# Fused linear attention and feed-forward layer on one core: w_in loaded in whole rows, batch loads issued by SyncE, the first batch spread over four engines

## The chip, the core and the metric

The kernel runs on one core of a Trainium2 chip. The metric is the device time of one execution in microseconds (us); the kernel before takes 349.92 us in the median of three runs (343.51 to 350.42). The engines are PE (TensorE, matmuls), DVE (VectorE), ACT (ScalarE), POOL (GpSimd) and SP (SyncE, which only issues transfers); PEld is PE's weight load.

## The reference

Eight batches with eight heads, 576 positions and 64 features per head go through a linear attention, and its 4608 rows of 512 features through a feed-forward layer with 2048 inner features:

```
theta = pi/2 * pos / 576
phi(x) = concat(relu(x) * cos(theta), relu(x) * sin(theta))        # 128 features
kv  = einsum('bhsf,bhsd->bhfd', phi(k), v);   z = sum_s phi(k)
x   = einsum('bhsf,bhfd->bhsd', phi(q), kv) / (phi(q) . z + 1e-6)
h   = x.transpose(0, 2, 1, 3).reshape(4608, 512) @ w_in             # 512 x 2048
out = (h * sigmoid(beta * h)) @ w_out                               # 2048 x 512
```

All inputs and the output are float32; the kernel multiplies in bf16.

## The kernel before, in words

The feed-forward layer runs over nine chunks of 512 rows (`c`), the attention over eight batches (`b`). The work is written out by hand in the order in which each engine shall take it; every engine executes its own instructions in that order and waits on semaphores. One chunk has 32 slots. Slots 0 to 15 are `h_group`: four matmuls into one of two PSUM banks, then one silu on ACT that writes `g_t`. Slots 16 to 31 are `o_part`: four matmuls each with `wout`, four parts to a 128-row output tile, which ACT copies out. Between the slots of chunk `c` the attention of batch `c + 1` is interleaved (`att_units`): relu of q, the turn of q by a transposing transfer (`q_turn_dma`, SP), relu of k, scaling of v by cosine and sine (`v_scale`), the tangent product of the turned q on POOL (`q_tan`), kv products (`kv_mm`) at slot 12, their copies out of PSUM (`kv_take`), num products (`num_mm`) and divisions (`x_div`) at slots 16, 18 and 20, and the turn of x into `xt` by transposing transfers on SP (`x_turn_dma`) one slot later each. DVE is not bound to the slots and runs ahead of PE. Chunk 0 carries batch 1 in the same way, with its turns on PE (the table `early`), and is a different order of the same steps: there the output parts go through all four row tiles before the next quarter of `wout`.

Batch 0 comes ahead of chunk 0; this stretch is called the head. The weights are loaded in it as well: four tiles of w_in and four of w_out, each 1.05 MB in float32, through four staging buffers (`w_stage`), so that a w_out load waits until a cast has emptied a buffer. The tile `win` wants its 512 input features in an order in which partitions 0 to 63 and 64 to 127 hold features of different heads. Before, `load_w` (lines 95 to 99) makes that order in the transfer: four transfers per tile, each of them into 64 partitions; `cast_w` then casts 128 partitions at once. A batch's q, k and v are 1.18 MB each, and two batches' tiles are held at a time (`raw_pool`).

Who issues: SP the first two batches and the weights, ACT the batches from 2 on. In lines 470 to 475 these issues stand on ACT at the start of a chunk; for batch 3 and on:

```
for c in range(1, NTC):
    if c + 2 < B:
        for name in "qvk":
            load_raw(c + 2, name, eng=nc.scalar)
```

A transfer that is issued takes one of eight semaphores in turn, and waits until the transfer that had that semaphore eight issues before has landed.

Of the kernel before, what the change touches and what calls it, by code (L numbers as in the profile page):

```python
# [10 lines left out]
FP32 = mybir.dt.float32  # L11
# [5 lines left out]
P = 128  # L17
# [5 lines left out]
def kernel(  # L23
# [60 lines left out]
    w_in_v = moe_w_in.rearrange("(jp jj g d) f -> jj d jp g f", jp=2, jj=2, g=2)  # L84
# [3 lines left out]
    def load_w(kind, i, f0=0, f1=512):  # L88
# [78 lines left out]
    xs = one.tile([P, 2, NQ, 2 * D], BF16, name="xs")  # L167
# [21 lines left out]
    def sel(jp):  # L189
        return slice(0, 4) if jp is None else slice(2 * jp, 2 * jp + 2)  # L190
# [31 lines left out]
    def q_turn_pe(b, jp, bank):  # L222
# [9 lines left out]
        for step in range(2):  # L232
            for e in range(2):
                i, n0, n1 = parts[e ^ step]
                if e == 0:
                    nc.scalar.copy(qt[:, jp, n0:n1], v2[i])  # L236
                else:
                    tan_mul(nc.vector, qs[:, jp, n0:n1], v2[i], n0, n1)
# [22 lines left out]
    def kv_take(b, jp, bank, both=False):  # L261
        t = kv_out(jp, bank)
        for g in range(2):
            for jj in range(2):
                rows = slice(jj * HP, (jj + 1) * HP)
                o = kv[rows, g, jp, :, jj * E : (jj + 1) * E]
                a = t[rows, g].rearrange("q (s e) -> q s e", s=2)
                if both and g == 1:
                    nc.scalar.copy(o, a)
                else:  # L270
                    nc.vector.tensor_copy(o, a)  # L271
# [242 lines left out]
```

## Time and profile before

| | before |
|---|---|
| median of 3 runs | 349.92 us (343.51 to 350.42) |
| profiled execution | 348.06 us, span 346.3 us |
| mean granted TensorE clock | 0.962 |
| PE busy | 306.4 us (88% of the span) |
| ACT, DVE, POOL busy | 136.2, 125.9, 73.5 us |
| moved by DMA | 53.60 MB |

The span is the time between the first and the last instruction of the profiled execution. "L339" is line 339 of the kernel before. In the chain and in timelines "ACTq" and "SPq" are the instruction queues of an engine while it issues transfers. A note such as [6.88 <-ACT g_t L343] says that the engine had been idle for 6.88 us just before, and that what it waited for was ACT's writing of g_t in line 343.

### The profile page before, as it was taken

Reading aid. Unit: us, or ns where it says so; the run is one execution under the profiler, and the core shown is the slowest. Engines: PE = TensorE matmul, PEld = TensorE weight load, DVE = VectorE, ACT = ScalarE, POOL = GpSimd, SP = SyncE. Lnnn points to the kernel's source line nnn. Section 1 sums busy time; section 2 is a strip of 40 time slices with the busy share of each in tenths; the row PEclk is TensorE's granted clock in tenths of the full one; section 3 lists DMA queues with packets and bytes.
Section 4 is the critical chain, followed back from the end, with each engine's and each line's share of the span. In section 5 each row is a group of like instructions: output and inputs, shape, how many; then the busy total and the mean of one; then the engine's idle time right before and its main releaser. Section 6 shows DMA issues by size and latency. Waiting matters only on the chain.

```text
span 346.3 us, 5863 instructions
## 1 busy us (share of the span) xinstructions
PE 306.4 (88%) x2363; PEld 146.2 (42%) x2390; DVE 125.9 (36%) x332; ACT 136.2 (39%) x209; POOL 73.5 (21%) x83
## 2 busy tenths in 40 slices
PE   5469958828999899979996999899999999999994
PEld 2354434413444345434542444345444544444441
DVE  3871479517239024802480058114902400000000
ACT  6437501505611661256113721463166127516711
POOL 2520000310233601342131503800370120000000
PEclk9789989976999999999998999999999999999998
DMA  7999990389618942595149706960640251032022
GB/s 276 266 217 256 389 377 12 88 306 389 228 37 154 316 163 50 112 305 204 39 105 253 276 18 129 273 251 17 133 112 3 49 113 30 0 70 53 0 60 61
DMA packets 50986, 53.60 MB, mean 155 GB/s; under 512 B 31232, under 2 KB 32272, under 8 KB 50960
## 3 DMA queue, kind: packets, MB, share of 16 engines
q1 hardware_dynamic: 38736, 24.65, 28.4%
q10 hardware_dynamic: 9536, 21.24, 16.7%
q0 software_dynamic: 2688, 7.34, 9.1%
q8 instruction: 18, 0.29, 0.4%
q14 instruction: 8, 0.07, 0.1%
HBM read 36.71 MB, written 9.44 MB: 133 GB/s over the span
## 4 chain that ended last, share of the span: by engine, by line
PE 68%; DMA 17%; ACTq 5%; DVE 3%; issue 2%; SPq 2%; ACT 1%; POOL 1%; POOLq 0%; DVEq 0%
PE ps L352 32%; PE ps L339 28%; DMA w_stage<-in_moe_w_out_dram 8%; PE ps L279 5%; ACTq L78 5%; DMA qt<-qb 4%; DMA raw_k<-in_k_dram 3%; DMA w_stage<-in_moe_w_in_dram 2%; PE ps L256 2%; SPq L97 1%; DVE wout L114 1%; DVE qs L218 1%; ACT g_t L343 1%; SPq L78 1%; POOL qs L218 1%
## 5 line engine op out<-in xcount | busy, mean ns | idle before, releaser
L339 PE MATMUL ps<-xt,win 128*128 128x512 bf16 x576 | 138.4, 387 | 15.4 <-ACT g_t L343 14.3
L352 PE MATMUL ps<-wout,g_t 128*128 128x512 bf16 x550 | 126.4, 380 | 2.5 <-issue 1.6
L343 ACT ACTIVATE g_t<-ps,beta 128x512 bf16<-128x512 f32 x144 | 98.4, 687 | 61.2 <-PE ps L339 47.7
L339 PEld LDWEIGHTS <-win 128*128 128x128 bf16 x576 | 56.3, 99 | 93.4 <-issue 35.9
L352 PEld LDWEIGHTS <-g_t 128*128 128x128 bf16 x576 | 54.6, 98 | 64.8 <-issue 1.2
L366 POOL DMA_DIRECT2D out_dram<-o_sb x56 | 36.2, 650 | 167.2 <-ACT o_sb L362 167.1
L362 ACT COPY o_sb<-ps 128x512 f32<-128x512 f32 x35 | 20.5, 586 | 108.8 <-PE ps L352 108.8
L271 DVE CAST kv<-ps 64x130 bf16<-64x130 f32 x60 | 17.5, 292 | 87.8 <-PE ps L256 86.8
L218 POOL TENSOR_TENSOR qs<-qt,tanr 128x1152 bf16<-128x1152 bf16 x12 | 28.3, 2378 | 35.7 <-DMA qt<-qb 26.9
L360 DVE COPY o_sb<-ps 128x256 f32<-128x256 f32 x1 | 0.4, 425 | 65.5 <-ACT o_sb L359 65.5
L295 DVE TENSOR_TENSOR xs<-ps,rden 128x768 bf16<-128x768 f32 (+1 forms) x27 | 23.4, 868 | 0.9
L279 PE MATMUL ps<-kv,qt 128*64 128x130 bf16 x288 | 21.2, 229 | 1.3 <-DVE kv L271 1.3
L279 PE MATMUL ps<-kv,qs 128*64 128x130 bf16 x288 | 20.6, 228 | 1.1 <-DVE qs L218 0.6
L279 PEld LDWEIGHTS <-qt 128*64 128x64 bf16 x288 | 16.4, 114 | 11.3 <-issue 10.5
L256 PE MATMUL ps<-vb,rk 64*64 64x130 bf16 x576 | 12.7, 235 | 7.6 <-ACT rk L194 4.0
L214 DVE TENSOR_SCALAR vb<-raw_v,cos 128x256 bf16<-128x256 f32 x63 | 17.1, 348 | 3.4 <-DMA raw_v<-in_v_dram 3.4
L279 PEld LDWEIGHTS <-qs 128*64 128x64 bf16 x288 | 16.7, 113 | 1.4 <-DVE qs L218 0.7
L214 DVE TENSOR_SCALAR vb<-raw_v,sin 128x256 bf16<-128x256 f32 x63 | 17.1, 349 | 0.0
L290 DVE TENSOR_TENSOR den<-ps,eps 128x12 f32<-128x12 f32 (+1 forms) x27 | 4.5, 168 | 32.1 <-PE ps L279 32.1
L256 PEld LDWEIGHTS <-rk 64*64 64x64 bf16 x576 | 10.1, 116 | 12.3 <-issue 6.4
L196 DVE TENSOR_SCALAR qb<-raw_q 128x1152 bf16<-128x1152 f32 x15 | 10.7, 753 | 8.1 <-DMA raw_q<-in_q_dram 8.1
L236 ACT COPY qt<-ps 128x640 bf16<-128x640 bf16 (+1 forms) x8 | 4.9, 640 | 22.1 <-PE ps L230 17.8
(51 smaller groups left out, 79.5 us busy)
## 6 DMA issues: line engine op xcount, KB each, us to landing
out_dram<-o_sb POOLq DMA_DIRECT2D x56, 128.0 KB, 2.9
raw_q<-in_q_dram ACTq DMA_DIRECT2D x6, 1152.0 KB, 7.7
raw_v<-in_v_dram ACTq DMA_DIRECT2D x6, 1152.0 KB, 10.5
raw_k<-in_k_dram ACTq DMA_DIRECT2D x6, 1152.0 KB, 12.3
w_stage<-in_moe_w_out_dram SPq DMA_DIRECT2D x4, 1024.0 KB, 14.1
w_stage<-in_moe_w_in_dram SPq DMA_DIRECT2D x12, 256.0 KB, 9.0
out_dram<-o_sb SPq DMA_DIRECT2D x16, 128.0 KB, 2.4
raw_q<-in_q_dram SPq DMA_DIRECT2D x2, 576.0 KB, 4.5
```

Of the source, the lines that this page charges most:

```text
L78: (eng or nc.sync).dma_start(out=raw_tile(b, name)[:, js].rearrange("q j n d -> q j (n d)"), in_=src.rearrange("(j g) (p n) d -> (g p) j ( ...
L214: nc.vector.tensor_scalar(vb[:, n, :, cs, 0:D], rv[:, :, n, :], scalar1=t[:, n : n + 1], scalar2=None, op0=ALU.mult)
L218: eng.tensor_tensor(dst.rearrange("q n (g p) -> q n g p", g=2), src.rearrange("q n (g p) -> q n g p", g=2), tanr[:, n0:n1].unsqueeze(2).to ...
L256: nc.tensor.matmul(t[jj * HP : (jj + 1) * HP, g], lhsT=rk[hs, n, 2 * jp + jj, :], rhs=vb[hs, n, 2 * jp + jj].rearrange("q s e -> q (s e)") ...
L271: nc.vector.tensor_copy(o, a)
L279: nc.tensor.matmul(ps[gs_, bank, i * 2 * E : (i + 1) * 2 * E], lhsT=(qt, qs)[cs][:, jp, n, gs_], rhs=kv[:, g, jp, cs, :], start=(cs == 0), ...
L295: nc.vector.tensor_tensor(xs[:, jps[0] : jps[-1] + 1, 3 * t : 3 * t + 3].rearrange("q s n (j d) -> q s (n j) d", j=2), nv[:, :, :, :, 0:D] ...
L339: nc.tensor.matmul(h_ps, lhsT=win[jt // 4][:, mi, (jt % 4) * P : (jt % 4 + 1) * P], rhs=xt[:, jp, :, g * HP : (g + 1) * HP], start=(mi == ...
L343: nc.scalar.activation(g_t, h_ps, AF.Silu, scale=beta[:, jt : jt + 1])
L352: nc.tensor.matmul(o_ps, lhsT=gs[c, jt][:, tt * P : (tt + 1) * P], rhs=wout[jt // 4][:, jt % 4, :], start=(jt == 0), stop=(jt == JT - 1))
L362: nc.scalar.copy(o_sb, o_ps)
L366: eng.dma_start(out=out_v[bb, n], in_=o_sb[hf * HP : (hf + 1) * HP, :])
```

## The change

- w_in: one transfer per tile, 128 rows at a time as they lie in memory, into 128 partitions. The order that `win` wants is made by the casts: four casts per tile, each of them from 64 partitions of the staging tile to 64 partitions of `win`, two of the four into the other half. Tile 0 is cast by POOL in eight pieces, tiles 1 and 2 by DVE in four, tile 3 by POOL in four (DVE before).
- Batch loads: all on SP. Batch 2 is issued in chunk 0, the others by `load_next` behind the q turn of the batch before.
- The last two w_out tiles are cast by ACT (six of eight pieces) and DVE (two), after the q turns of batch 1.
- `xs` and `xt` have the two column halves (jp) side by side in each block of 64 rows, so that one transfer turns both; the moving operand of the h products changes with it (`xt[:, :, jp, ...]`).
- `kv_take`: two copies for all four parts, in place of eight.
- The head: 29 warm-up matmuls in place of nine; k's relu on ACT ahead of a qt copy, k's second half loaded and cut in two pieces; the first copies of kv on ACT; division of nine blocks at once, its last third on ACT; xt copies on DVE and ACT.

```diff
-    w_in_v = moe_w_in.rearrange("(jp jj g d) f -> jj d jp g f", jp=2, jj=2, g=2)
+    w_in_v = moe_w_in.rearrange("(j p) f -> p j f", p=P)
...
-        for jj in range(2):
-            for jp in range(2):
-                nc.sync.dma_start(
-                    out=st[jj * HP : (jj + 1) * HP, 2 * jp : 2 * jp + 2, f0:f1],
-                    in_=w_in_v[jj, :, jp, :, i * 512 + f0 : i * 512 + f1])
...
+        nc.sync.dma_start(out=st, in_=w_in_v[:, :, i * 512 : (i + 1) * 512])
+
+    def cast_win(i, gj, eng="dve", f0=0, f1=512):
+
+        g, jj = gj
+        o = win[i].rearrange("q (jp g) f -> q jp g f", g=2)[jj * HP : (jj + 1) * HP, :, g, f0:f1]
+        a = stages["in", i].rearrange("q (jp jj) f -> q jp jj f", jj=2)[g * HP : (g + 1) * HP, :, jj, f0:f1]
...
-    xs = one.tile([P, 2, NQ, 2 * D], BF16, name="xs")
+    xs = one.tile([P, NQ, 2, 2 * D], BF16, name="xs")
...
-            xts[c] = xt_pool.tile([P, 2, NB, P], BF16, name="xt", tag="xt")
+            xts[c] = xt_pool.tile([P, NB, 2, P], BF16, name="xt", tag="xt")
...
+    def kv_take(jps, bank, jjs=(0, 1), gs_=(0, 1), eng="dve"):
+        a0, a1 = jps[0], jps[-1] + 1
+        for jj in jjs:
+            rows = slice(jj * HP, (jj + 1) * HP)
+            o = kv[rows, gs_[0] : gs_[-1] + 1, a0:a1, :, jj * E : (jj + 1) * E]
+            a = ps[rows, bank + gs_[0] : bank + gs_[-1] + 1, a0 * 2 * E : a1 * 2 * E]
...
     def x_turn_dma(b, t):
         for c, o, n0, n1 in pieces(b, t):
-            for jp in range(2):
-                nc.sync.dma_start(out=xt_tile(c)[:, jp, o : o + n1 - n0], in_=xs[:, jp, n0:n1].rearrange("q n c -> q (n c)"),
-                                  transpose=True)
+            nc.sync.dma_start(out=xt_tile(c)[:, o : o + n1 - n0].rearrange("q n s c -> q (n s) c"),
+                              in_=xs[:, n0:n1].rearrange("q n s c -> q (n s c)"), transpose=True)
...
-                             rhs=xt[:, jp, :, g * HP : (g + 1) * HP],
+                             rhs=xt[:, :, jp, g * HP : (g + 1) * HP],
...
+    warm_pe(13)
+    take("act", 0)
+    v_scale(0, 1, 0, eng="pool")
+    v_scale(0, 0, 0)
+    k_relu(0, 0, 2, "act")
+    take("dve", 1)
+    take("dve", 0)
+    take("act", 1)
+    kv_mm(0, 0, 6)
...
+    x_rden(1, 0)
+    x_mul(1, 0, 0, 1)
+    x_mul(1, 0, 1, 2)
+    for n in range(6, NQ):
+        x_mul_act(1, 0, n)
+    for f in (0, 256):
+        for gj in GJ:
+            cast_win(0, gj, "pool", f, f + 256)
...
-    cast_w("in", 2)
+    for gj in GJ:
+        cast_win(2, gj)
     load_w("out", 2)
-    cast_w("in", 3)
+    for gj in GJ:
+        cast_win(3, gj, "pool")
     load_w("out", 3)
...
+        13: lambda: (v_scale(1, 0), [v_scale(1, 1, jp, eng="pool") for jp in range(2)]),
+        17: lambda: k_relu(1),
+        20: lambda: (kv_mm(1, 0, 6), kv_mm(1, 1, 6), q_relu(1, 0), kv_take((0, 1), 6), q_relu(1, 1)),
+        22: lambda: q_turn_pe(1, 0, 4),
+        23: lambda: (q_turn_pe(1, 1, 6), cast_wout(2, "aaaa"), cast_wout(3, "aadd")),
...
+        def load_next():
+            for name in "qvk":
+                if b + 1 < B:
+                    load_raw(b + 1, name)
+
         u = [
-            (0, lambda: (q_relu(b, 0), q_relu(b, 1))),
+            (0, lambda: (q_relu(b, 0), q_relu(b, 1), q_turn_dma(b), load_next())),
             (1, lambda: v_scale(b, 0)),
-            (1, lambda: q_turn_dma(b)),
...
+        if slot == 24:
+            for name in "qvk":
+                load_raw(2, name)
...
-    for name in "qvk":
-        load_raw(2, name, eng=nc.scalar)
     for c in range(1, NTC):
-        if c + 2 < B:
-            for name in "qvk":
-                load_raw(c + 2, name, eng=nc.scalar)
```

How the rows of two engines move. On ACT, between two chunks (line 343 or 381 is the silu, 362 or 400 the copy of an output tile, 321 or 360 the copy of a turned x). Before:

```order
L343 ACTIVATE g_t<-ps,beta 128x512 x16
L362 COPY o_sb<-ps 128x512 x4
L78 DMA raw_q<-in_q_dram 128x4x576
L78 DMA raw_v<-in_v_dram 128x4x576
L78 DMA raw_k<-in_k_dram 128x4x576
```

Now, from the end of chunk 0 on:

```order
L400 COPY o_sb<-ps 128x512 x2
L360 COPY xt<-ps 128x256
L360 COPY xt<-ps 128x512
L381 ACTIVATE g_t<-ps,beta 128x512 x16
L400 COPY o_sb<-ps 128x512 x4
```

No issue of a transfer stands between a chunk's copies and the next chunk's silu instructions any more.

On SP, from the first loads to the last w_out load (a piece of the difference; 64x2x512 is 64 partitions with two pieces of 512):

```order
 L78 DMA raw_v<-in_v_dram 128x2x576
-L78 DMA raw_k<-in_k_dram 128x2x576
-L97 DMA w_stage<-in_moe_w_in_dram 64x2x256 x8
-L97 DMA w_stage<-in_moe_w_in_dram 64x2x512 x12
+L78 DMA raw_k<-in_k_dram 128x576 x2
+L95 DMA w_stage<-in_moe_w_in_dram 128x4x512 x4
 L93 DMA w_stage<-in_moe_w_out_dram 128x4x512 x2
+L78 DMA raw_v<-in_v_dram 128x4x576
 L78 DMA raw_k<-in_k_dram 128x4x576
-L78 DMA raw_v<-in_v_dram 128x4x576
 L78 DMA raw_q<-in_q_dram 128x4x576
 L93 DMA w_stage<-in_moe_w_out_dram 128x4x512 x2
```

Twenty transfers of w_in have become four, and batch 1's v has gone ahead of its k. The same place of the changed program with the semaphores that each row waits for (DMAHW4 and so on are the eight semaphores of transfers, Pool counts POOL's instructions):

```order
L95 DMA w_stage<-in_moe_w_in_dram 128x4x512 [waits DMAHW3_49]
L93 DMA w_stage<-in_moe_w_out_dram 128x4x512 [waits DMAHW4_49,DMAHW0_49,Pool_49]
L93 DMA w_stage<-in_moe_w_out_dram 128x4x512 [waits DMAHW5_49,DMAHW3_49,Pool_49]
L78 DMA raw_v<-in_v_dram 128x4x576 [waits DMAHW6_49]
L78 DMA raw_k<-in_k_dram 128x4x576 [waits DMAHW7_49]
```

The first of the two w_out loads takes the buffer of w_in tile 0 and waits for POOL's last cast of it. The second takes the buffer of w_in tile 3 (DMAHW3 is that tile's load) and waits for POOL's last cast of tile 3; before, the second one waited for a cast on DVE.

## Rows read from the trace of the kernel before

**Rows 1.** The page, part 1: span, busy time per engine.
```profile
span 346.3 us, 5863 instructions
PE 306.4 (88%) x2363; PEld 146.2 (42%) x2390; DVE 125.9 (36%) x332; ACT 136.2 (39%) x209; POOL 73.5 (21%) x83
```

**Rows 2.** Busy time by stage: length, engines, PE clock, DMA share, GB/s.
```profile
25.67:70.07 44.40, 37.47 (x305) 18.56 (x309) 25.96 (x61) 17.86 (x29) 3.92 (x8) 0.96 0.70 221
70.07:252.06 181.99, 165.91 (x1346) 77.97 (x1361) 76.29 (x211) 66.01 (x100) 50.62 (x49) 0.96 0.63 180
252.06:284.54 32.48, 32.22 (x271) 15.37 (x272) 6.40 (x17) 13.34 (x20) 8.91 (x10) 1.00 0.30 67
```

**Rows 3.** The chain of waits from 250 us on: start, length, what.
```profile
263.97 1.15 PE ps L256 x72
...
274.12 0.82 PE ps L279 x24
...
284.54 14.63 PE ps L339 x64
...
299.22 10.74 PE ps L352 x49
```

**Rows 4.** Timeline, starts of chunks 1, 2 and 4: start, length, instruction.
```profile
75.31 2.74 ACTq L78 DMA_DIRECT2D raw_k<-in_k_dram  x1
...
78.83 12.75 PE L339 MATMUL ps<-xt,win 128*128 128x512 bf16 x44 [6.88 <-ACT g_t L343]
...
115.67 1.67 PE L339 MATMUL ps<-xt,win 128*128 128x512 bf16 x7 [1.12 <-ACT g_t L343]
...
186.04 1.23 PE L339 MATMUL ps<-xt,win 128*128 128x512 bf16 x4 [2.81 <-ACT g_t L343]
```

**Rows 5.** Busy time in stretches of the first 51 us, columns as in rows 2.
```profile
0.00:4.00 4.00, 0.00 (x0) 0.00 (x0) 1.39 (x7) 2.71 (x4) 2.19 (x11) 1.00 0.45 144
4.00:11.00 7.00, 6.15 (x29) 3.50 (x29) 3.51 (x8) 4.28 (x8) 2.12 (x1) 1.00 1.03 394
12.00:16.00 4.00, 1.21 (x37) 1.09 (x39) 3.23 (x5) 1.86 (x3) 1.78 (x1) 0.58 1.07 207
18.00:31.00 13.00, 10.13 (x136) 6.15 (x133) 7.93 (x22) 6.40 (x11) 1.09 (x2) 0.94 1.05 223
34.00:51.00 17.00, 13.38 (x87) 5.93 (x90) 10.75 (x28) 5.43 (x8) 0.00 (x0) 0.98 1.05 389
```

**Rows 6.** Timeline of SP: the first w_out loads.
```profile
25.62 1.63 SPq L93 DMA_DIRECT2D w_stage<-in_moe_w_out_dram  x2
```

**Rows 7.** Timeline of the head and of chunk 0.
```profile
11.40 2.38 POOL L208 TENSOR_TENSOR vb<-raw_v,sin 128x1152 bf16<-128x1152 f32 x1 [0.81 <-DMA raw_v<-in_v_dram]
...
14.46 1.19 PE L256 MATMUL ps<-vb,rk 64*64 64x130 bf16 x36 [4.01 <-ACT rk L194]
...
48.84 1.30 PE L256 MATMUL ps<-vb,rk 64*64 64x130 bf16 x20 [3.51 <-DVE vb L214]
...
51.80 1.68 DVE L114 TENSOR_SCALAR wout<-w_stage,rbeta 128x512 bf16<-128x512 f32 x4 [0.91 <-DMA w_stage<-in_moe_w_out_dram]
...
69.10 0.51 PE L315 MATMUL ps<-ident,xs 128*128 128x128 bf16 x6 [0.56 <-DVE xs L295]
```

**Rows 8.** The tile qt: its transposing transfers from issue to landing.
```profile
DMA to landing us min/median/max: 5.5/7.2/15.4
```

**Rows 9.** Groups of instructions, 0 to 26 us: count, busy us, mean ns, idle before.
```profile
L208 POOL TENSOR_TENSOR vb<-raw_v,sin 128x1152 bf16<-128x1152 f32 x2 | 4.5, 2247 | 6.2 <-DMA raw_v<-in_v_dram 6.2
L295 DVE TENSOR_TENSOR xs<-ps,rden 128x384 bf16<-128x384 f32 x6 | 3.3, 558 | 0.2
...
L108 POOL CAST win<-w_stage 128x1024 bf16<-128x1024 f32 x2 | 2.4, 1184 | 3.0 <-DMA w_stage<-in_moe_w_in_dram 2.9
...
L110 DVE CAST win<-w_stage 128x2048 bf16<-128x2048 f32 x1 | 1.2, 1227 | 0.0
...
L321 ACT COPY xt<-ps 128x512 bf16<-128x512 bf16 x1 | 0.6, 586 | 0.1
```

More of the change, by code (lines that the diff above doesn't have):

```diff
@@ L231, in q_turn_pe, with take @@
                                  is_transpose=True, start=(n == n0), stop=(n == n1 - 1))
[L232 to L238, printed above, removed]
+        def take(e, i):
+            _, n0, n1 = parts[i]
+            if e == "act":
+                nc.scalar.copy(qt[:, jp, n0:n1], v2[i])
+            else:
+                tan_mul(nc.vector, qs[:, jp, n0:n1], v2[i], n0, n1)
+        if hold:
+            return take
+        for e, i in (("act", 0), ("dve", 1), ("act", 1), ("dve", 0)):
+            take(e, i)
     def q_turn_dma(b):
@@ L248, in kv_out, with kv_mm @@
         return ps[:, bank : bank + 2, jp * 2 * E : (jp + 1) * 2 * E]
-    def kv_mm(b, jp, bank):
+    def kv_mm(b, jp, bank, jjs=(0, 1)):
         t = kv_out(jp, bank)
         for n in range(NQ):
-            for jj in range(2):
+            for jj in jjs:
                 for g in range(2):
@@ L259, in kv_mm @@
                         start=(n == 0), stop=(n == NQ - 1))
[L261 to L271, printed above, removed]
+    def kv_take(jps, bank, jjs=(0, 1), gs_=(0, 1), eng="dve"):
+        a0, a1 = jps[0], jps[-1] + 1
+        for jj in jjs:
+            rows = slice(jj * HP, (jj + 1) * HP)
+            o = kv[rows, gs_[0] : gs_[-1] + 1, a0:a1, :, jj * E : (jj + 1) * E]
+            a = ps[rows, bank + gs_[0] : bank + gs_[-1] + 1, a0 * 2 * E : a1 * 2 * E]
+            o = o.rearrange("q g s c e -> q g (s c) e")
+            a = a.rearrange("q g (s e) -> q g s e", e=E)
+            if eng == "act":
+                nc.scalar.copy(o, a)
+            else:
+                nc.vector.tensor_copy(o, a)
     def num_mm(b, t, jp, bank):
@@ L299, in x_div, with x_rden, x_mul @@
             op=ALU.mult)
+    rdens = {}
+    def x_rden(jp, bank):
+        nv = x_sums(bank, 3)
+        den = small.tile([P, 3, 3, 2], FP32, name="den3", tag="den3")
+        nc.vector.tensor_tensor(
+            den, nv[:, :, :, :, D],
+            eps9.rearrange("q (t i) -> q t i", t=3).unsqueeze(3).to_broadcast([P, 3, 3, 2]), op=ALU.add)
+        rdens[jp] = small.tile([P, 3, 3, 2], FP32, name="rden3", tag="rden3")
+        nc.vector.reciprocal(rdens[jp], den)
+    def x_mul(jp, bank, t0, t1):
+        nv = x_sums(bank, 3)
+        nc.vector.tensor_tensor(
+            xs[:, 3 * t0 : 3 * t1, jp].rearrange("q n (j d) -> q n j d", j=2),
+            nv[:, t0:t1, :, :, 0:D].rearrange("q t i j d -> q t (i j) d") if t1 - t0 > 1 else nv[:, t0, :, :, 0:D],
+            rdens[jp][:, t0:t1].rearrange("q t i j -> q (t i) j").unsqueeze(3).to_broadcast([P, 3 * (t1 - t0), 2, D]),
+            op=ALU.mult)
@@ L301, in pieces, with x_mul_act @@
+    def x_mul_act(jp, bank, n):
+        t, i = divmod(n, 3)
+        nv = x_sums(bank, 3)
+        for jj in range(2):
+            nc.scalar.activation(xs[:, n, jp, jj * D : (jj + 1) * D], nv[:, t, i, jj, 0:D], AF.Copy,
+                                 scale=rdens[jp][:, t, i, jj : jj + 1])
     def pieces(b, t):
@@ L400 @@
[L400 to L413 removed]
+    for t in range(3):
+        num_mm(0, t, 0, 3 + t)
@@ new lines @@
+    kv_mm(0, 1, 6, (0,))
+    kv_mm(0, 1, 6, (1,))
+    warm_pe(3, bank=1)
+    x_rden(0, 3)
+    x_mul(0, 3, 0, 3)
+    kv_take((1,), 6, eng="act")
+    for t in range(3):
+        num_mm(0, t, 1, t)
+    warm_pe(3, bank=6)
+    x_rden(1, 0)
[6 more added lines that the diff above has]
+            cast_win(0, gj, "pool", f, f + 256)
+    x_turn_pe(0, 0, 6, ("dve",))
+    x_turn_pe(0, 1, 7, ("act",))
```

185 lines of the change are left out of this document (82 added, 103 removed).

## The prediction

> **What bounds the kernel now.** I read the page first: the span is 346.3 us and PE is busy for 306.4 us of it [rows 1]. The profiled execution took 348.06 us, so 1.76 us lie outside the span; the median of the runs is 349.92 us, 0.5% above it, and I make the sum against 348.06.
>
> Then the span by stages, cut where a chunk's first h product may start [rows 2]. Chunk 6 (252.06 to 284.54) has the attention of a batch beside it and no load of a batch: 32.48 us, PE busy 32.22. That is PE's own work, as the chain shows: 64 h products in 14.63 us, 72 kv products in 1.15, three times 24 num products in 0.82, and the o products at 10.74 us for 49 [rows 3], 14.0 for 64; together 32.3. Chunks 1 to 5 do the same work in 181.99 us, which is 36.4 each. So they lose 181.99 - 5 x 32.48 = 19.6 us. The head (up to 25.67) and chunk 0 (44.40 us, PE busy 37.47) lose the rest.
>
> What chunks 1 to 5 wait for stands in the timeline of their starts [rows 4]. ACT issues the batch loads in front of the chunk's silu instructions. At the start of chunk 1 six loads keep ACT's queue until 75.31 + 2.74 = 78.05, and PE's next h product waited 6.88 us for g_t, since it has only two PSUM banks for h. In chunk 2 the same wait is 1.12 us, in chunk 4 it is 2.81. A stall is followed by a lower clock: the 44 h products from 78.83 take 12.75 us, against 14.63 for 64 in [rows 3].
>
> The head and chunk 0 are set by transfers, seen in four windows [rows 5]. The batch's first tiles arrive at 394 GB/s, w_out and batch 1 at 389, but the w_in pieces between them at 207 to 223, with the DMA engines equally busy (1.03 to 1.07). The w_in pieces are the ones that write 64 partitions each. They hold back what stands behind them on SP: the first w_out load is issued at 25.62 [rows 6]. In chunk 0 PE then waits 3.51 us for batch 1's v, and the cast of the third w_out tile starts only at 51.80, on landing [rows 7].
>
> **The change, part by part.**
> *Batch loads from ACT to SP.* ACT loses 18 issues, SP gains 18, and loses 22 transposes (44 become 22, each for both column halves). Batch 2's loads now stand right behind the last w_out load, those of batch c+2 behind batch c+1's q transpose. Who is behind them on SP: the xt transposes of slots 17, 19 and 21, and through them the next chunk's h products. The q transpose is asked for as soon as DVE is through with the last batch's divisions, near slot 21, and lands in 5.5 to 15.4 us [rows 8]; the loads behind it are 3.54 MB, 9.1 us at 389 GB/s. From slot 21 to the next chunk's slot 17 are 28 slots, some 28 us, so both end 3 to 13 us before the next xt transpose, and the move costs nothing; if that cover went, each chunk would lose what the transpose is late. PE's 32.48 us stay: 5 x 32.48 in place of 181.99, **-19.6 us**. Bounds: 0 (a new wait takes all) and -20.6 (32.3 us a chunk from the chain).
>
> *w_in in whole rows.* 4.19 MB at 223 GB/s are 18.8 us, at 389 they are 10.8: the stream of transfers ends 8 us earlier, if whole rows move like w_out's. Between 223 and 389 I take 389, since w_out tiles have the same 128 partitions and 2 KB pieces; 223 goes to a rival.
>
> *The casts.* A cast now covers 64 partitions and reads one half while it writes the other. No row shows such a cast. Price by elements per partition: POOL 1184 ns for 1024, DVE 1227 ns for 2048 [rows 9]. Below: nothing beyond the four quarter casts at these rates; above: twice that, if 64 lanes or the crossing cost as much again. I take the first, the nearest row. POOL then needs 8 x 0.59 = 4.7 us for tile 0 and 4 x 1.18 = 4.7 us for tile 3; DVE 2.5 us each for tiles 1 and 2.
>
> *A new wait.* The second w_out load waits, by the order, for POOL's last cast of w_in tile 3. Behind it on SP stand batch 1, w_out 2 and 3, and batch 2. Working: 0.58 MB of the batch are in at 4.0 us (144 GB/s [rows 5]), the rest of 3.54 MB at 394 GB/s by 11.5, the four w_in tiles by 22.3, the first w_out tile by 25.0. A tile lands about 1.4 us after its last byte (estimate: v's second half, due at 10.0 us by the same rate, let POOL start at 11.40 [rows 7]). Tile 3 lands at 23.7, POOL is through at 28.4, bytes flow again at about 29.5, so the stream idles 4.5 us. The remaining 6.68 MB end at 46.7 and land by 48.1. Before, the cast of 51.80 still had a tile behind it: some 5 us gained, not 8.
>
> *The head.* Before, the first kv product waited for rk until 14.46, since ACT took k after its qt copies [rows 7]; now k goes ahead of one, and 13 warm products fill the wait. I expect kv at 12.0 and the products after it at full clock (it was granted 0.58 between 12 and 16 [rows 5], near its lower level, 1.2 GHz). The pair of kv copies per bank, the nine-block divisions (558 ns per three blocks before [rows 9]) and the spread over ACT and DVE save and add about the same. First h product at 23.0 in place of 25.67: **-2.7 us**. Bounds: 0 (the added instructions eat it) and -4 (kv's gain and the clock in full). POOL's casts of tile 0 end at 15.6 + 4.7 = 20.3, before it.
>
> *Chunk 0.* With the first h product at 23.0, PE reaches kv of batch 1 (slot 20) at 23.0 + 14.6 + 5 x 0.89 = 42.0. Batch 1's k lands at 39.7 and POOL's two sine products (2247 ns each [rows 9]) are done at 41.1, so the 3.51 us wait goes. Late next is w_out tile 2: it lands at 45.5, but ACT casts it behind the four qt copies, which PE releases at 45.7 and 47.3; with a DVE step between two of them they end at 48.6, and four casts at 0.59 (ACT's 128x512 copy takes 586 ns [rows 9]) end at 51.0. PE stands at slot 24 from 47.3: 3.7 us. From there 8 x 0.89 of o, 2.5 of num, 1.5 of transposes (three times 0.51 [rows 7]) and 0.6 for a last xt copy give 62.7. Chunk 0 becomes 39.7 us: **-4.7 us**. Bounds: 0 (casts doubled, POOL holding SP) and -8 (no stall at slot 24).
>
> Sum: -19.6 - 2.7 - 4.7 = -27.0, a span of 319.3 and, with the 1.76 us outside, **321.1 us**.
>
> **A rule weighed.** POOL's tile 3 (23.7 to 28.4) and DVE's eight casts of tiles 1 and 2 (from about 24) meet here for the first time: in the trace before, the POOL cast of 1184 ns [rows 9] ran beside DVE instructions that read PSUM. The Trainium skill's "SBUF — State Buffer" (section "Who interferes with whom") says that a VectorE cast in its two-port mode and a GpSimd instruction exclude each other, the loser waiting for the whole instruction; no row here shows it. By the rows the sum is 321.1; by that rule it is rival A's figure.
>
> **The rivals.**
> A. POOL is late: its casts wait for DVE's, or crossing halves costs. For: no row shows either. Against: POOL has only those casts to do there. If all 4.9 us of DVE's casts come in between, or tile 3's casts double, the second w_out load and all behind it come 4.8 us later, and chunk 0 with them: 326.
> B. Whole rows change nothing for w_in, since its rows stay 8 KB apart in HBM, and that, not the 64 partitions, made 223 GB/s. For: w_out and the batches are contiguous in HBM. Against: half of 389 is close to the 207 to 223 seen, which fits a half of something. Tile 3 then lands 8 us later, PE waits some 3 us for it at slot 12, chunk 0 ends at about 72: 72 + 6 x 32.48 + 61.8 (346.3 - 284.54) + 1.8 = 331. The skill's page named above (section "Can I just issue two DMAs to hit both halves?") says that one transfer over all 128 partitions is what reaches every port; that speaks against B.
> C. The wait moves from ACT to SP: loads stand ahead of transposes, and a chunk's xt or qt is late. For: a q transpose took 15.4 us once [rows 8]. Against: it has 15.8 us to slot 16 beyond its head start. If it costs 4 us in each of five chunks: 341, no change that can be told.
> D. Slower: xt now has both column halves side by side, so the h products' moving operand steps 512 bytes between its 128-byte runs, not 256. If that slowed PE's reading, 576 products would pay. To pass 357 from 321 they need +62 ns each (now 14.63 / 64 = 229); it decides from there on. Against: o products read one contiguous run and take 219 [rows 3], so runs with gaps already cost nearly nothing. At +70 ns: 361.
> E. Better: chunk 0 and the head at their lower bounds, -8 and -4: 316.5, or 315.5 with the chunks at 32.3.
>
> **The numbers.** Chances: forecast 0.62, A 0.18, B 0.07, C 0.05, D 0.02, E 0.06. The likeliest is 321.1 us. Its own range is 317 to 326 (above, the head's or chunk 0's gain lost, 2.7 or 4.7; below, most of chunk 0's stall gone). A and B reach to 331, E down to 315; with a microsecond or two at either end for what a term is misjudged by, 314 to 333. The cases in it hold 0.93 by their chances, and I count on some 0.85, for what is unnamed. A measurement here tells some 2% apart, 343 to 357. Faster by more: the forecast, A, B, E and a part of C, 0.95. Within: the rest of C and small losses, 0.03. Slower: D, 0.02.
>
> **What would show it.** In the changed profile: chunks 1 to 5 at 32.5 us each, no wait of h products for g_t over 1 us, no batch load on ACT; w_in at 380 GB/s or more; the first h product near 23; a gap of 4 to 5 us in the transfers before the second w_out tile, its length telling the forecast from A; a PE wait of 3 to 4 us near 47 us for w_out tile 2's casts on ACT. Wrong would be: chunks still at 34 or more, w_in near 220 GB/s, or h products over 240 ns.

## The result: 328.5 us in place of 348.4, with 7.4 us left behind the forecast in one stretch

Timed side by side, the changed kernel takes 328.5 us (median; 328.32 to 329.4) and the kernel before 348.38. The ratio is 0.9522 [0.9438, 0.9605]. The forecast was 321.1. The profiled execution took 329.4 us, 1.9 of it outside the span. Spans below are of one profiled execution each; where the median of the times tells another size, it stands beside.

The page of the changed kernel, part 1, against [rows 1]:

```profile
span 327.5 us, 5827 instructions
PE 309.5 (94%) x2410; PEld 147.3 (45%) x2410; DVE 122.3 (37%) x267; ACT 141.3 (43%) x220; POOL 87.2 (27%) x95
```

The span lost 18.8 us and PE's busy time did not fall: what went was waiting. The same cut by stages as [rows 2], at each chunk's first h product (head, chunk 0, chunks 1 and 5, the last two chunks; length, engines, PE clock, DMA share, GB/s):

```profile
0.00:22.15 22.15, 19.25 (x214) 11.12 (x215) 15.69 (x30) 13.04 (x26) 11.57 (x21) 1.00 0.93 339
22.15:70.50 48.35, 38.38 (x308) 19.23 (x309) 31.91 (x52) 21.37 (x35) 12.80 (x12) 0.89 0.69 248
70.50:103.10 32.60, 32.60 (x273) 15.46 (x273) 17.61 (x47) 13.19 (x20) 11.78 (x11) 1.00 0.80 214
...
200.50:233.00 32.50, 32.50 (x274) 15.33 (x272) 12.79 (x32) 13.33 (x20) 10.27 (x10) 1.00 0.56 170
...
265.50:327.50 62.00, 56.88 (x256) 24.71 (x254) 0.42 (x1) 27.04 (x41) 1.03 (x2) 1.00 0.17 39
```

| stage | before | forecast | measured |
|---|---|---|---|
| head | 25.67 | 23.0 | 22.15 |
| chunk 0 | 44.40 | 39.7 | **48.35** |
| chunks 1 to 5 | 181.99 | 162.4 | 162.50 |
| chunk 6 | 32.48 | 32.48 | 32.50 |
| chunks 7, 8 | 61.76 | 61.76 | 62.00 |

Every stage is within 0.9 us of its forecast but chunk 0, which was to fall by 4.7 us and rose by 3.95. It is the only stage here whose clock is under 1 (0.89).

The chain of waits of the changed kernel, its first 60 us, tells chunk 0's story in one column (start, length, what; only the stretches named below):

```profile
10.27 15.48 DMA w_stage<-in_moe_w_in_dram
25.80 1.24 POOL win L105
...
29.97 1.15 POOL win L105
...
31.14 0.37 SPq L93
...
31.56 8.43 DMA raw_v<-in_v_dram
40.02 6.16 DVE vb L220 x9
46.18 1.28 DVE rk L197
47.50 2.17 PE ps L265 x69
...
55.61 2.46 ACT wout L114 x4
58.11 2.29 PE ps L390 x5
```

Read downwards: w_in's tile 3 arrives; POOL casts it until 31.12; only then does batch 1's v leave; DVE scales v by the cosine for 6.16 us; then k's relu; then PE may start kv at 47.50. PE had been ready since 40.96 and stood for 6.54 us. Later it stands for ACT's casts of w_out's third tile. Why v left so late is on SP's queue, and beside DVE's cosine stands a POOL group (timelines of PE, SP and POOL, changed kernel):

```profile
47.50 2.17 PE L265 MATMUL ps<-vb,rk 64*64 64x130 bf16 x72 [6.54 <-DVE rk L197]
...
56.28 0.38 PE L390 MATMUL ps<-wout,g_t 128*128 128x512 bf16 x1 [2.11 <-ACT wout L114]
...
21.49 10.02 SPq L93 DMA_DIRECT2D w_stage<-in_moe_w_out_dram  x2
...
25.80 5.31 POOL L105 CAST win<-w_stage 64x1024 bf16<-64x1024 f32 x4 [4.34 <-DMA w_stage<-in_moe_w_in_dram]
...
40.15 4.30 POOL L210 TENSOR_TENSOR vb<-raw_v,sin 128x1152 bf16<-128x1152 f32 x2 [9.04 <-DMA raw_v<-in_v_dram]
```

SP stands 10.02 us in its first two w_out loads: the second leaves at 31.14, behind POOL's last cast, with batch 1 and every later load behind it. The transfers (windows, columns as above) show it as a hole between two full stretches:

```profile
12.00:15.00 3.00, 2.68 (x65) 1.62 (x64) 3.00 (x4) 1.89 (x4) 2.40 (x1) 1.00 1.05 394
15.00:20.00 5.00, 4.66 (x100) 3.21 (x94) 3.76 (x8) 1.03 (x5) 3.51 (x6) 1.00 1.05 387
...
30.00:34.00 4.00, 4.00 (x19) 1.74 (x18) 2.18 (x4) 2.92 (x5) 1.11 (x1) 1.00 0.33 119
34.00:45.00 11.00, 6.96 (x32) 2.91 (x30) 6.66 (x9) 2.75 (x4) 4.30 (x2) 0.97 1.03 385
45.00:56.00 11.00, 6.67 (x102) 4.33 (x103) 8.36 (x16) 2.85 (x5) 0.00 (x0) 0.72 1.05 390
```

The w_in tiles now move at 387 to 394 GB/s, against 207 to 223 in [rows 5]. The last row's clock of 0.72 is what PE got after standing still: the 72 kv products take 2.17 us, and 1.15 in [rows 3].

**The theory after the result.** Chunk 0 lost to one chain: (a) the second w_out load waits for POOL's casts of tile 3; (b) POOL and DVE hold each other up, in those casts and again in cosine and sine; (c) ScalarE's w_out casts are queued behind its copies of q's turn. **Rivals**: that casts across the partition halves are slow in themselves; that w_in's layout in HBM counts; that PE is slower on the new xt; that the moved loads only shifted a wait.

### The profile page after: what moved, and what is told of

Its sections match the earlier page's. It is cut to its first block, busy times and chain, and to the rows that moved or that the text cites. A ratio compares the mean times of both kernels' runs of the same rounds, so it can differ in the third digit from the quotient of the medians.

```text
span 327.5 us, 5827 instructions
## 1 busy us (share of the span) xinstructions
PE 309.5 (94%) x2410; PEld 147.3 (45%) x2410; DVE 122.3 (37%) x267; ACT 141.3 (43%) x220; POOL 87.2 (27%) x95
## 4 chain that ended last, share of the span: by engine, by line
PE 82%; DMA 9%; DVE 3%; POOL 2%; SPq 1%; ACT 1%; issue 0%; ACTq 0%; DVEq 0%
PE ps L390 38%; PE ps L377 36%; PE ps L289 5%; DMA w_stage<-in_moe_w_in_dram 5%; PE ps L265 3%; DMA raw_v<-in_v_dram 3%; DVE vb L220 2%; POOL win L105 2%; DMA raw_q<-in_q_dram 2%; SPq L95 1%; ACT wout L114 1%; DVE qs L223 1%; DVE rk L197 0%; PE ps L354 0%; ACT o_sb L400 0%
## 5 line engine op out<-in xcount | busy, mean ns | idle before, releaser
L390 PE MATMUL ps<-wout,g_t 128*128 128x512 bf16 x576 | 132.4, 383 | 2.8 <-ACT wout L114 2.8
L377 PE MATMUL ps<-xt,win 128*128 128x512 bf16 x576 | 133.9, 378 | 1.2 <-ACT xt L360 1.2
L404 POOL DMA_DIRECT2D out_dram<-o_sb x56 | 37.7, 678 | 151.9 <-ACT o_sb L400 151.9
L281 DVE CAST kv<-ps 64x520 bf16<-64x520 f32 x14 | 9.8, 698 | 79.8 <-PE ps L265 79.7
L223 POOL TENSOR_TENSOR qs<-qt,tanr 128x1152 bf16<-128x1152 bf16 x12 | 28.4, 2386 | 5.0 <-PE ps L377 4.9
L220 DVE TENSOR_SCALAR vb<-raw_v,cos 128x256 bf16<-128x256 f32 x63 | 20.8, 405 | 1.7 <-DMA raw_v<-in_v_dram 1.7
L307 DVE TENSOR_TENSOR xs<-ps,rden 128x768 bf16<-128x768 f32 x21 | 20.1, 957 | 0.7
L302 DVE TENSOR_TENSOR den<-ps,eps 128x12 f32<-128x12 f32 x21 | 3.6, 170 | 40.5 <-PE ps L289 40.5
L265 PE MATMUL ps<-vb,rk 64*64 64x130 bf16 x576 | 11.4, 230 | 6.7 <-DVE rk L197 6.5
L220 DVE TENSOR_SCALAR vb<-raw_v,sin 128x256 bf16<-128x256 f32 x54 | 14.7, 348 | 0.0
L210 POOL TENSOR_TENSOR vb<-raw_v,sin 128x1152 bf16<-128x1152 f32 x4 | 8.8, 2213 | 15.9 <-DMA raw_v<-in_v_dram 15.9
```

The source lines that it names most:

```text
L210: (nc.gpsimd if eng == "pool" else nc.vector).tensor_tensor(vb[:, n0:n1, js, cs, 0:D], rv.rearrange("q j n d -> q n j d")[:, n0:n1, js], t ...
L220: nc.vector.tensor_scalar(o, a, scalar1=t[:, n : n + 1], scalar2=None, op0=ALU.mult)
L223: eng.tensor_tensor(dst.rearrange("q n (g p) -> q n g p", g=2), src.rearrange("q n (g p) -> q n g p", g=2), tanr[:, n0:n1].unsqueeze(2).to ...
L265: nc.tensor.matmul(t[jj * HP : (jj + 1) * HP, g], lhsT=rk[hs, n, 2 * jp + jj, :], rhs=vb[hs, n, 2 * jp + jj].rearrange("q s e -> q (s e)") ...
L307: nc.vector.tensor_tensor(xs[:, 3 * t : 3 * t + 3].rearrange("q n s (j d) -> q s n j d", j=2), nv[:, :, :, :, 0:D], rden.unsqueeze(4).to_b ...
L377: nc.tensor.matmul(h_ps, lhsT=win[jt // 4][:, mi, (jt % 4) * P : (jt % 4 + 1) * P], rhs=xt[:, :, jp, g * HP : (g + 1) * HP], start=(mi == ...
```

## The experiments

Times are medians; ratios are to the kernel before, run beside each. "c0" is the stretch from the first h product of chunk 0 to that of chunk 1.

**1. Tile 3 on VectorE.**

```
         cast_win(3, gj, "pool")   ->   cast_win(3, gj)
```

> The changed kernel with w_in tile 3 cast by DVE, not POOL; by the order the second w_out load then waits for DVE's cast of tile 1, not for POOL's of tile 3. Theory (chunk 0 grew because SP stood behind POOL's casts from 25.80 to 31.12 us with batch 1 behind it): the second w_out load is issued near 24.5 and not 31.14, v of batch 1 lands near 36 and not 40.0, kv of batch 1 starts near 43 and not 47.5; span 323 (-4.5 us from 327.5). Rival (DVE's own work sets chunk 0, since DVE now has 2.8 us more of casts): kv stays near 47 and the span within 1 us of 327.5.

Measured: 320.62 us, ratio 0.9259 [0.9209, 0.9308], span 319.2, 8.3 less. SP, DVE and PE in its timeline:

```profile
21.71 3.19 SPq L93 DMA_DIRECT2D w_stage<-in_moe_w_out_dram  x2
...
34.15 6.17 DVE L220 TENSOR_SCALAR vb<-raw_v,cos 128x256 bf16<-128x256 f32 x9 [0.67 <-DMA raw_v<-in_v_dram]
...
41.64 1.22 PE L265 MATMUL ps<-vb,rk 64*64 64x130 bf16 x72 [0.90 <-DVE rk L197]
```

SP's stand is 3.19 us in place of 10.02, v arrives 5.9 us earlier, kv starts 5.86 earlier at full clock, and c0 is 40.20. About half of that had been forecast, 4.5 us. kv starts 1.4 us before the 43 that I had expected, and I had not counted the clock that comes back: kv and the eight o products behind it take 1.22 and 1.90 us in place of 2.17 and 2.70.

All twelve casts of DVE, by their line (shortest, median and longest in ns):

```profile
L107 DVE CAST win<-w_stage x12: 675/689/692, 21.7 to 29.5; 64x1024 bf16<-64x1024 f32 x12
```

At the rate of the full-width cast in [rows 9], 2048 columns in 1227 ns, the 1024 columns of one cast would take 613; their mean of 687 is some 12% more. Six of the twelve cross the partition halves and six stay in theirs, yet all lie between 675 and 692. So the 12% are not the crossing, and that rival falls.

One thing the edit does on the side: the ring of staging buffers now deals the second w_out load another buffer, that of tile 1. Experiment 9 takes the two apart.

**2. Sine on VectorE.**

```
-13: (v_scale(1, 0), [v_scale(1, 1, jp, eng="pool") for jp in range(2)]),
+13: (v_scale(1, 0), v_scale(1, 1)),
```

> The changed kernel with batch 1's sine products on DVE, as in the kernel before, not on POOL. Theory (DVE and POOL shut each other out of SBUF: nine cosine products took 6.16 us beside POOL and 2.45 alone): cosine takes 2.45 us, sine 2.45 after it, kv starts near 46.3 in place of 47.5, span 326.3. Rival (the cosine products were slow for their landing, packet by packet, or for the clock): they take 6 us again, sine comes on top, kv at 50, span 330.

Measured: 326.65 us, ratio 0.9429 [0.9376, 0.9483], span 323.4, 4.1 less. DVE in its timeline:

```profile
39.05 2.45 DVE L220 TENSOR_SCALAR vb<-raw_v,cos 128x256 bf16<-128x256 f32 x9 [1.78 <-DMA raw_v<-in_v_dram]
41.42 2.45 DVE L220 TENSOR_SCALAR vb<-raw_v,sin 128x256 bf16<-128x256 f32 x9
43.78 1.35 DVE L197 TENSOR_SCALAR rk<-raw_k 128x2304 bf16<-128x2304 f32 x1
```

The nine cosine products take 2.45 us alone, right behind v's landing, and 6.16 beside POOL: DVE lost 3.71 us to 4.30 us of POOL's work, which itself ran no slower than in [rows 9] (4.30 us for two, against 2247 ns each). In the changed kernel one single cosine product took 2203 ns, about the length of one POOL instruction, with a median of 346:

```profile
L220 DVE TENSOR_SCALAR vb<-raw_v,cos x63: 341/346/2203, 40.0 to 228.2; 128x256 bf16<-128x256 f32 x63
```

Doing both products on one engine is done 1.3 us sooner than sharing them between two. The span fell by 4.1 us where 1.2 had been forecast; by the medians it is 1.85 (326.65 against 328.5). kv starts 2.3 us earlier in this trace: 1.3 are the products, and 1.0 is v's landing, since POOL's casts of tile 3 ended 1.0 us earlier in this execution, which the edit does not touch. The rest is kv and the o products behind it at full clock.

**3. Batch loads back on ScalarE.** `load_raw(c + 2, ...)` at the places of the kernel before, the rest as changed.

```
-            (0, lambda: (q_relu(b, 0), q_relu(b, 1), q_turn_dma(b), load_next())),
+            (0, lambda: (q_relu(b, 0), q_relu(b, 1), q_turn_dma(b))),
...
+        if c + 2 < B:
+            for name in "qvk":
+                load_raw(c + 2, name, eng=nc.scalar)
```

> The changed kernel with the batch loads from batch 2 on back on ACT at the places of the kernel before. Theory (ACT's queue at the chunk starts was the whole loss of chunks 1 to 5): chunks 1 to 5 lose 15 to 20 us again, span 343 to 347, waits of h products for g_t of 1 to 7 us. Rival (the gain came from the merged transposes, the shorter kv copies and the steadier order as well): less than 10 us come back, span under 338.

Measured: 343.57 us, ratio 0.9912 [0.9884, 0.9939], span 342.1. Its chunk 1 begins:

```profile
72.54 4.19 ACTq L78 DMA_DIRECT2D raw_v<-in_v_dram  x1
...
76.75 2.77 ACTq L78 DMA_DIRECT2D raw_k<-in_k_dram  x1
...
80.31 12.72 PE L377 MATMUL ps<-xt,win 128*128 128x512 bf16 x44 [8.04 <-ACT g_t L381]
```

The picture of [rows 4] is back: two loads hold ScalarE's queue for 7 us, PE waits 8.04 us, and 44 products run at the lower clock. Chunk 1 takes 43.81 us; chunks 2 to 5 some 33.3 each. Undoing the move costs 14.6 us of span, just under the 15 to 20 forecast. Chunks 1 to 5 take 177.1 us here (280.02, where chunk 6 ends, less 70.39 and 32.5) and 181.99 in [rows 2], with the loads on the same queue; which other part of the change gives these 4.9 us was not separated.

**4. Each w_in transfer in two halves of 64 partitions.**

```
-        nc.sync.dma_start(out=st, in_=w_in_v[:, :, i * 512 : (i + 1) * 512])
+        for hf in range(2):
+            hs = slice(hf * HP, (hf + 1) * HP)
+            nc.sync.dma_start(out=st[hs], in_=w_in_v[hs, :, i * 512 : (i + 1) * 512])
```

> The changed kernel with each w_in transfer cut in two by partition halves: the same rows of HBM, the same 2 KB pieces, 64 partitions per transfer. Theory (64 partitions per transfer made the old loads slow): 210 to 225 GB/s between 12 and 30 us, tile 3 lands near 34 and not 25.8, PE waits for it at slot 12, span 329 to 333. Rival (the old order of rows, or their number of transfers, made it): 380 GB/s or more, span within 1 us of 327.5 or below, since by the order the second w_out load waits for DVE here.

Measured: 331.25 us, ratio 0.9569 [0.9492, 0.9646], span 329.4. Its windows:

```profile
12.00:16.00 4.00, 3.42 (x108) 2.75 (x108) 2.90 (x5) 1.43 (x3) 3.21 (x2) 1.00 1.07 221
18.00:31.00 13.00, 10.31 (x68) 4.62 (x63) 8.24 (x14) 8.00 (x16) 3.66 (x6) 1.00 1.05 216
```

Same bytes, same rows in HBM, 216 to 221 GB/s. It is the 64 partitions, and not that the transfers are shorter: batch 0's first loads, of about the same size but into 128 partitions, move at 394 [rows 5]. Rival B's pitch in HBM is refuted. The span is only 1.9 us longer (2.75 by the medians, of two runs here), but that is not the price of the rate alone. The edit also deals the second w_out load another buffer. SP's and POOL's timelines show it:

```profile
22.84 3.59 SPq L93 DMA_DIRECT2D w_stage<-in_moe_w_out_dram  x2
...
31.89 2.11 POOL L107 CAST win<-w_stage 64x1024 bf16<-64x1024 f32 x2 [9.08 <-DMA w_stage<-in_moe_w_in_dram]
34.40 2.12 POOL L107 CAST win<-w_stage 64x1024 bf16<-64x1024 f32 x2 [0.39 <-DMA w_stage<-in_moe_w_in_dram]
```

The load is out at 26.4, long before POOL casts tile 3. Experiment 9 has such a load at the full rate. These four casts of POOL take 4.23 us while DVE is idle; in the changed kernel, with DVE casting beside them, the same four took 5.31.

**5. The loads' move alone**, in the kernel before.

```
+        def load_next():
+            for name in "qvk":
+                if b + 1 < B:
+                    load_raw(b + 1, name)
...
-            (1, lambda: q_turn_dma(b)),
+            (1, lambda: (q_turn_dma(b), load_next())),
...
+        if slot == 24:
+            for name in "qvk":
+                load_raw(2, name)
...
-        if c + 2 < B:
-            for name in "qvk":
-                load_raw(c + 2, name, eng=nc.scalar)
```

> The kernel before with one part of the change alone: the batch loads of chunks 0 to 5 issued by SyncE (batch 2 in chunk 0's slot 24, batch c+2 behind batch c+1's q transpose). By the prediction's term: chunks 1 to 5 at 32.5 us each, 19.6 us less, a span near 326.7 and a time near 328.5, with head and chunk 0 as before (25.7 and 44.4). By the run that put the loads back on ScalarE, which cost 14.6 us: the same move is worth 14 to 15 here, a time of 333. Rival (the whole rows and casts are what shortened the steady chunks): over 340.

Measured: **328.37 us**, ratio 0.9497 [0.9447, 0.9548], span 327.4. Its stages:

```profile
0.00:26.02 26.02, 14.53 (x193) 9.32 (x195) 17.27 (x43) 11.92 (x21) 9.04 (x15) 0.93 0.94 249
26.02:70.68 44.66, 38.51 (x304) 18.90 (x308) 27.14 (x63) 17.85 (x29) 3.91 (x7) 0.92 0.91 300
70.68:103.20 32.52, 32.26 (x270) 15.39 (x273) 20.05 (x58) 13.19 (x20) 10.15 (x10) 1.00 0.73 185
```

The forecast's -19.6 term, by itself, to the tenth: span 18.9 less, chunks 1 to 6 at 32.4 to 32.5 each. It also says what the other two parts of the change came to with the buffers as they were dealt: **nothing**. They shortened the head by 3.9 us (26.02 to 22.15) and lengthened chunk 0 by 3.7 (44.66 to 48.35).

**6. w_out's third tile ahead of the copies.**

```
-22: q_turn_pe(1, 0, 4),
-23: (q_turn_pe(1, 1, 6), cast_wout(2, "aaaa"), cast_wout(3, "aadd")),
+22: (cast_wout(2, "aaaa"), q_turn_pe(1, 0, 4)),
+23: (q_turn_pe(1, 1, 6), cast_wout(3, "aadd")),
```

> The changed kernel, with ScalarE's four casts of w_out's third tile put ahead of the four copies of the q turns. Theory (PE stands at slot 24 for those casts, 2.1 us and three times 0.23, because they are queued behind the copies): the wait goes, and the span falls by 2 to 2.8 us, from 327.5 to about 325. Rival (the tile itself lands too late, or the copies that now come later hold the num products): under 0.7 us less.

Measured: 323.39 us, ratio 0.9343 [0.9302, 0.9384], span 322.0, 5.5 less (5.1 by the medians): twice the forecast. The casts now follow their landing (47.87 to 50.43) and the wait at slot 24 is gone. Windows from kv to the next chunk tell where the rest is from (first the changed kernel, then this one; c0 42.98):

```profile
47.50:56.28 8.78, 6.67 (x103) 4.33 (x103) 6.14 (x10) 3.13 (x6) 0.00 (x0) 0.79 1.05 390
56.28:62.00 5.72, 5.01 (x34) 2.29 (x34) 0.36 (x3) 3.00 (x5) 0.00 (x0) 0.70 0.54 199
```

```profile
46.62:52.00 5.38, 5.05 (x85) 3.30 (x87) 2.77 (x4) 2.56 (x4) 0.00 (x0) 0.57 1.05 389
52.00:65.02 13.02, 12.09 (x141) 7.26 (x141) 10.14 (x22) 7.67 (x14) 3.33 (x6) 1.00 0.70 238
```

After the kv wait both run at a low clock. In the changed kernel the second stand (2.1 us at 56.28, waits of 0.23 behind it) leaves the next 5.7 us at 0.70 too; without it everything from 52.00 on is at 1.00. And kv itself came 0.9 us earlier, with tile 3's casts (24.82 to 30.56 here). That leaves 4.6 us behind kv: 2.8 of waits and 1.8 that go with the clock.

**7. and 8. The two VectorE edits together, without and with the casts moved ahead.**

> Both earlier edits together: w_in's tile 3 cast on VectorE and batch 1's sine products on VectorE, so that GpSimd touches neither beside VectorE. Theory: cosine and sine take 2.45 us each from the landing of v (near 34.2), k's relu ends near 40.5, PE's wait of 0.9 us before the kv products goes, and no more: a span 0.7 to 1.2 us under the 319.2 of the first edit alone, 318 to 318.5, a time near 320. Rival (the two locks cost PE twice what the kv wait shows): under 316.

> Tile 3 and the sine on VectorE, and w_out's third tile cast ahead of the q turns' copies. Theory: the terms add, 0.9 for kv and 2 to 2.8 for slot 24, a span of 315.5 to 316.5 and a time near 317.5. Rival (with kv earlier, PE reaches slot 24 before the tile has landed): 318 to 320.

Measured: 319.91 us, ratio 0.9245 [0.9204, 0.9286], span 318.1, c0 39.46; and 315.64 us, ratio 0.9123 [0.9081, 0.9166], span 314.6, c0 35.53. In the first, kv starts with no wait and gains what was forecast, 1.1 us of span (0.7 by the medians). In the second kv starts at 40.78, and its windows from there to chunk 1 are:

```profile
40.78:46.00 5.22, 5.06 (x105) 3.48 (x106) 3.10 (x5) 3.02 (x5) 0.00 (x0) 1.00 1.05 389
46.00:52.00 6.00, 5.44 (x65) 2.94 (x65) 5.40 (x11) 3.00 (x6) 0.00 (x0) 1.00 1.05 390
52.00:57.59 5.59, 4.82 (x56) 3.05 (x55) 4.03 (x11) 3.98 (x8) 3.33 (x6) 1.00 0.56 155
```

No wait, no fall of the clock from kv to chunk 1. The casts' place is worth 3.5 us more here (4.3 by the medians), again above 2 to 2.8: a stretch of 6.6 us at 0.74 that followed the wait in the first of the two is gone with it.

**9. Other buffers, same casts.** Tile 3 stays on GpSimd; only the staging buffers are dealt out otherwise: each w_out tile takes the buffer of the w_in tile with its number.

```
+    for i in range(4):
+        stages["out", i] = stages["in", i]
     load_w("out", 0)
     load_w("out", 1)
```

> The changed kernel with its casts as they are, tile 3 on GpSimd included; only the staging buffers are dealt out otherwise: w_out's tile i goes into the buffer of w_in's tile i, so that the second w_out load waits for VectorE's casts of tile 1 and no longer for GpSimd's casts of tile 3. Theory (the lateness of tile 3's casts harmed only through the buffer that the second w_out load was dealt): that load is issued near 25, v right behind it, the kv products come at 41.6 to 42.5 (cosine and sine still meet and take 6.2 us), a span of 319.5 to 321, as when VectorE cast the tile. Rival (GpSimd's casts beside VectorE's are what costs, whatever the buffer): kv later than 44 and a span over 323.

Measured: 320.13 us, ratio 0.9258 [0.9207, 0.9308], span 318.0. SP, POOL and PE in its timeline:

```profile
21.10 3.61 SPq L93 DMA_DIRECT2D w_stage<-in_moe_w_out_dram  x2
...
25.38 5.31 POOL L105 CAST win<-w_stage 64x1024 bf16<-64x1024 f32 x4 [4.31 <-DMA w_stage<-in_moe_w_in_dram]
...
41.34 1.22 PE L265 MATMUL ps<-vb,rk 64*64 64x130 bf16 x72 [0.80 <-DVE rk L197]
...
48.36 0.38 PE L390 MATMUL ps<-wout,g_t 128*128 128x512 bf16 x1 [2.11 <-ACT wout L114]
...
50.20 1.24 PE L390 MATMUL ps<-wout,g_t 128*128 128x512 bf16 x5 [0.23 <-ACT wout L114]
```

POOL's casts are as slow as in the changed kernel (5.31 us) and nobody cares: c0 is 39.28. Two lines that touch no computation are worth 9.5 us of span, 8.4 by the medians. What hurt was not who cast tile 3 but that the second w_out load had been dealt tile 3's buffer, the last to come free; with tile 1's it was out at 24.7. PE's stand at slot 24 is still there, but the clock does not fall behind it: five o products take 1.24 us, and 2.29 in the changed kernel after the same waits.

This is also the run to set beside experiment 4: the second w_out load is free early in both, and w_in moves at half the rate there. The spans are 318.0 and 329.4 us, c0 39.28 and 51.18. With the buffer out of the way, the whole rows are worth about 11 us; the two runs also differ in the buffers of other loads, which was not separated.

**10. Other buffers, sine on VectorE, casts ahead.** Experiment 9 with the edits of 2 and 6.

> The same dealing of the buffers, with batch 1's sine products on VectorE and w_out's third tile cast ahead of the q turns' copies; tile 3 stays on GpSimd. Theory: as good as the version with tile 3 on VectorE, a span of 314.3 to 316 and a time near 317, since from slot 20 on PE waits for nothing. Rival (VectorE's and GpSimd's casts in turn still hold up w_in's tile 2 or the second w_out load): 317 to 319.

Measured: 315.71 us, ratio 0.9137 [0.9091, 0.9182], span 314.1, c0 35.52: the same as experiment 8 within the runs. These two are the best versions, some 13 us under the changed kernel and 30 to 31 under the one before.

## Why the prediction was right, and where it failed

- **Batch loads to SP, -19.6: right.** Chunks 1 to 5 take 162.5 us, the loads on SP delayed no transpose, and experiment 5 reaches it with this part alone. Rival C is out.
- **Whole rows at 389 GB/s: right** (387 to 394), and by experiment 4 for the reason given. Rival B is out. What it is worth hung on the buffer of the second w_out load: see the last paragraph of this section.
- **The head, -2.7: right and a little more**, -3.5. kv came at 12.59 us (12.0 forecast), and from 12 to 20 us nothing fell below full clock where [rows 5] had 0.58. w_in's rate has no part in it: in experiment 4 the head is 21.39 us.
- **Chunk 0, -4.7: wrong in sign, +3.95.** The steps were named in the right order, with wrong sizes. POOL's casts of tile 3 were to run from 23.7 to 28.4 and ran from 25.80 to 31.12. Of the 2.7 us that they ended late, 2.1 are their start and 0.6 their length. The start waits for tile 3's landing, by the trace at 25.75 in place of 23.7; in the other runs with these loads and casts they start at 24.4 to 25.4, and why the landing varies stays open. v was due at 36.6 and was there at 40.0. Then the step that failed most, an overlap that I had put at nothing: DVE's cosine was taken at 2.45 us and took 6.16, beside a POOL group that the prediction itself had put at the same time. rk was due near 41.1 and came at 47.45; 3.4 of these 6.4 us are v's landing and 3.7 the cosine, less 0.7 that k's landing would have cost anyway. The other 2.3 us of the 8.65 are behind kv, from kv to the next chunk 23.0 us in place of 20.7, although the wait at slot 24 was 0.9 shorter than forecast: that is the clock, which the prediction left out. PE is busy for 38.38 us of chunk 0 here at a mean clock of 0.89, and for 35.06 in experiment 9 at 1.00.
- **The wait at slot 24, 3.7 us: mechanism right**, 2.8 measured, and 2.1 to 2.8 in experiments 1, 2, 4, 7 and 9 as well, whenever kv came. It is smaller because the prediction had PE wait for the last of the four casts, and the o products take them one by one: 2.11 us for the first, 0.23 for each of the others. Its price was more than its length, because of the clock.
- **Rival A came about in kind, not in size.** It had a chance of 0.18, and that its 326 us lies near 328.5 is luck. It had POOL's casts hold everything up by 4.8 us. They did so by 2.7, of which 2.1 are the landing; beside DVE's casts they took 5.31 us against 4.23 without (experiment 4), and crossing halves cost nothing that experiment 1 shows. The larger share is DVE's cosine, which A did not name. It was right to weigh the rule of the Trainium skill's "SBUF — State Buffer" (section "Who interferes with whom") and wrong to apply it only to the casts. The trace agrees with it: DVE lost 3.71 of the 4.30 us that POOL worked, and a cast of DVE that takes 688 ns alone took up to 1434 beside POOL. The Trainium skill's page says that the loser waits for a whole instruction. Here one cosine product took 2203 ns where POOL's were 1.2 to 2.2 us long, and DVE has nine short ones, each of which can lose.
- **D is out**: 64 h products of chunk 0 take 14.49 us, 14.63 in [rows 3]; their mean over the run is 378 ns, and 387 before with its stretches at a lower clock.

```profile
L377 PE MATMUL ps<-xt,win 128*128 128x512 bf16 x576 | 133.9, 378 | 1.2 <-ACT xt L360 1.2
```

The last part of the account is that w_in's faster transfers bought nothing in the kernel as it stands: they ended earlier into a hole, since the load behind them stood waiting for a buffer. With the buffers dealt in order (experiment 9) the hole is gone, v comes 6 us earlier, PE waits 0.80 for kv, and chunk 0 takes 39.28 us. That this is the 39.7 of the forecast is luck: the forecast had a hole of 4.5 us and a cosine of 2.45, and here there is no hole and the cosine takes 6.17. So of the two causes the buffer is the larger, and with it removed the faster transfers are worth some 11 us of span against experiment 4.

## What to carry to other kernels

When a transfer gets faster, look at what is queued behind it on the issuing engine and which buffer that load will be given: a ring that hands out the buffer freed last turns the gain into a hole, and two lines that tie buffers by hand can decide whether the faster transfer is worth anything. When an experiment slows one thing, check that it did not move another: experiment 4 alone would have priced w_in's rate at 1.9 us. Before spreading work over VectorE and GpSimd, list every pair that will run at the same time, not only the one just moved; sharing cosine and sine between the two was slower than one engine doing both. And a stall of PE can cost more than its length, by the low clock after it: removing 2.3 to 2.8 us of waits at slot 24 gave 3.5 us in experiment 8 and 4.6 in experiment 6.

## What the runs showed that was not expected

- VectorE's nine scaling products of 128x256 took 2.45 us alone and 6.16 to 6.17 beside 4.30 us of GpSimd's, in six kernels; GpSimd's took no longer than in [rows 9].
- Casts of 64x1024 beside each other cost both engines: GpSimd's took 1291 ns in the mean and 1036 without VectorE's (experiment 4), VectorE's 870 ns and 687 without GpSimd's (experiment 1).
- A cast between partition halves cost no more than one within a half: 675 to 692 ns for 64x1024 on VectorE, some 12% over the full-width rate in both cases. On GpSimd 64x512 took 609 ns, against 592 by the rate of [rows 9].
- ScalarE's scaled copy of 128x512 from the staging buffer took 712 ns (2.56 us for four in a row), a plain copy of that size out of PSUM 586.
- After a stand of 2.1 us at slot 24, with up to three waits of 0.23 behind it, PE's mean granted clock was 0.70 to 0.74 for the next 6 us in five kernels (the changed one and experiments 1, 2, 4 and 7), between its levels of 1.2 and 2.4 GHz. In experiment 9 it stayed at 1.00 after the same stand and waits. What decides it is open.
